# Seven-product gate in two more token groups of a fused attention and SwiGLU kernel, with stores and the q weighting moved to other engines

## The chip, the cores and the metric

The kernel runs on one core of a Trainium2 chip. The metric is the device time of one execution in microseconds (us); the time before is the median of three runs. The profile is of one execution, and its times count from the span's start.

## What is computed

A linear attention (cosformer) over 8 batches, 8 heads, 576 positions and 64 features is followed by a SwiGLU feed-forward block over the resulting 4608 tokens of 512 features. Cut to what matters:

```python
def phi(x, c, s):                      # c, s: cosine and sine of the position, per position
    r = np.maximum(x, 0.0)
    return np.concatenate([r * c, r * s], axis=-1)
q_p, k_p = phi(q, cos_w, sin_w), phi(k, cos_w, sin_w)
kv = np.einsum('bhsf,bhsd->bhfd', k_p, v)
z = np.sum(k_p, axis=2)
num = np.einsum('bhsf,bhfd->bhsd', q_p, kv)
den = np.einsum('bhsf,bhf->bhs', q_p, z)[..., None] + 1e-06
x = (num / den)                        # heads joined: 4608 tokens x 512
g = x @ w_gate                         # 512 x 1536
h = g / (1 + np.exp(-g)) * (x @ w_val) # w_val: 512 x 1536
out = h @ w_out                        # 1536 x 512
```

## The kernel before

The tokens are worked through in nine groups (0 to 8) of 512 tokens. A group has an FFN stage (12 chunks of 128 hidden features: gate and value products, silu, multiplication) and an output stage. Work for later groups is put into slots between the chunks: 12 slots in the FFN stage (0 to 11) and 4 in the output stage (12 to 15). Batch b's q, k and v are prepared so that its key-value products run in slot 5 of group b - 1, and each group's four token tiles (the attention result x and its transposition xT) are made during the group before.

PSUM is eight banks that the program hands out itself with `take` and `give_back`; a helper may take a bank that an earlier user has still to be read from, and then TensorE waits.

A plain group's chunk:

```python
def ffn_mm(...):
    for i in which:                    # gate, then value
        for kc in range(KC):           # 4 matmuls of 512 tokens each
            nc.tensor.matmul(out=..., lhsT=(wg_sb, wv_sb)[i][:, kc, fs], rhs=xT[tg][:, ts, kc], ...)
```

Groups in `GATE` (7 and 8 before) compute the gate by a scheme with seven block products in place of eight (of the Strassen-Winograd kind), in three thirds u of four chunks each. It needs weight sums (made once, `gate_weight_sum`), differences of xT (`x_sum`, in the output stage of the group before) and additions of partial results:

```python
def product(to, u, a, x, first):       # 4 matmuls of 256 tokens
    ...
for u in range(3):
    product(a, u, A11, B11, True)
    b = bank("b", seeded=True)
    nc.scalar.copy(out=b, in_=a)                                        # seeds bank b
    product(e, u, W3, X3, True)
    nc.scalar.copy(out=m7, in_=e)
    V(...); done()                     # V: value product of a chunk; done: a slot
    product(b, u, W2, X2, False)
    nc.vector.tensor_tensor(out=c, in0=m7, in1=b, op=ALU.add)           # L659
    product(a, u, A12, B21, False); silu(u, 1, 0, a)
    mul(...); V(...); done()
    product(b, u, W1, X1, False)
    nc.vector.tensor_tensor(out=m7, in0=m7, in1=b, op=ALU.add)          # L668
    silu(u, 0, 1, m7)
    product(c, u, A22, X4, False); silu(u, 0, 0, c)
    V(...); done()
    # ... mul x2, token sums in the last third
    product(b, u, W4, B22, False); silu(u, 1, 1, b)
    # ... V, mul, done, and the token sum S3 (second third) or S4 (last third)
```

Here `product` is L621, `V` is L633, `silu` is L627 and `mul` is L638. The output stage of groups 2 to 8 (`out_by_quarters`, matmuls L786) is a scheme of the same kind, with seven products of 12 matmuls of 256 columns, in the order a, e, b, slot 12, a, slot 13, b, c, slot 14, b, slot 15. It uses the sums S1 to S4 of the hidden values, made by VectorE (`token_sum`, L760). Its third b product needs S4, and VectorE to have read bank b for the quarter C22 (L827).

The preparation of q on ScalarE and VectorE, and the copies of the key-value result:

```python
def phi_q(b, g):                       # one of 4 head pairs
    relu_op("act", o, o)                                                # ScalarE, L266
    nc.vector.tensor_tensor(out=st[b, "q"][:, g], in0=o..., in1=tab, op=ALU.mult)   # VectorE, L283
def vmul(b, g):                        # v weighted by cosine and sine, VectorE, L287
def qturn_dma(b, e):                   # DMA transpose of st[b, "q"] (tile r_q, one buffer) into phit
    nc.sync.dma_start_transpose(...)
def kv_out2(b):                        # four copies PSUM to SBUF, L356
    for w, eng in enumerate((nc.scalar.copy, nc.vector.tensor_copy)): ...
def store(t, cols=..., queues=None):   # two stores of a tile's rows
    (queues or (nc.sync, nc.sync))[e].dma_start(...)
def load_behind(b):
    nc.gpsimd.tensor_copy(out=hold2, in_=phit[b - 1][0:1, :, 0, 0, 0])  # waits for the turned q of b - 1
    load(b, "q")
    if b > 3:
        load_kv(b)
```

Loads are issued from GpSimd's queue; stores and DMA transposes are issued from SyncE's queue, in program order.

Of the kernel before, what the change touches and what calls it, by code (L numbers as in the profile page):

```python
# [18 lines left out]
def kernel(  # L19
# [29 lines left out]
    HT = T // 2  # L49
    HD = d_model // 2  # L50
    KH = KC // 2
    GATE = (7, 8)

    consts = ctx.enter_context(tc.tile_pool(name="consts", bufs=1))
    raw = ctx.enter_context(tc.tile_pool(name="raw", bufs=2))
# [221 lines left out]
    def phi_q(b, g):  # L277

        if g == 0:
# [3 lines left out]
        nc.vector.tensor_tensor(out=st[b, "q"][:, g], in0=o.unsqueeze(2).to_broadcast([P, NC, 2, D]),  # L283
                                in1=tab, op=ALU.mult)

    def vmul(b, g):
        nc.vector.tensor_tensor(  # L287
            out=v2s[b == 1][:, g, :, :, 0:D],
            in0=(first if b == 0 and g == 0 else {"v": raw_of(b, "v")})["v"][:, g].unsqueeze(2).to_broadcast([P, NC, 2, D]),
            in1=tab, op=ALU.mult,  # L290
        )
# [59 lines left out]
    def kv_out2(b):  # L351

        ps = st[b, "kvps"][:, :, 0:4 * J * D1 // 2].rearrange("p e (j w x) -> p e j w x", j=J, w=2)
        for w, eng in enumerate((nc.scalar.copy, nc.vector.tensor_copy)):
            for i in range(2):
                eng(out=kv2s[b % 2][w * D:(w + 1) * D, :, :, i], in_=ps[i * D:(i + 1) * D, :, :, w])  # L356

# [249 lines left out]
    def ffn_by_quarters(tg, slot_of):  # L607
# [37 lines left out]
        for u in range(3):  # L645
            a = bank("a", fills=True)
            product(a, u, A11, B11, True)
            b = bank("b", seeded=True)
            nc.scalar.copy(out=b, in_=a)
            e = bank("e", fills=True)  # L650
            product(e, u, W3, X3, True)
            m7 = m7p.tile([P, 2, HT], FP32, name="m7")
            nc.scalar.copy(out=m7, in_=e)
            free("e")
            V(*((u - 1, 1, 1) if u else (u, 0, 0)))
            done()
            product(b, u, W2, X2, False)
            c = bank("c", seeded=True)
            nc.vector.tensor_tensor(out=c, in0=m7, in1=b, op=ALU.add)  # L659
            product(a, u, A12, B21, False)  # L660
            silu(u, 1, 0, a)
            free("a")
            if u:
                mul(u - 1, 1, 1)
            V(u, 0, 0) if u else V(u, 1, 0)
            done()
# [3 lines that stand above are left out]
            product(c, u, A22, X4, False)  # L670
            silu(u, 0, 0, c)
            free("c")
            V(u, 1, 0) if u else V(u, 0, 1)
            done()
            if u == 2:
                for n in (1, 2):
                    token_sum(n, 0, 4)
            mul(u, 0, 0)
            mul(u, 1, 0)
            if u == 2:  # L680
                token_sum(3, 4, 6)
            product(b, u, W4, B22, False)
            silu(u, 1, 1, b)
            free("b")
            if u:
                V(u, 0, 1)
            mul(u, 0, 1)
            if u:
                done()
                token_sum(*((3, 0, 4) if u == 1 else (4, 0, 4)))  # L690
        V(2, 1, 1)
        mul(2, 1, 1)
        for n in (1, 2):
# [73 lines left out]
    def out_by_quarters(tg, slot_of):  # L767

        last = tg == NTG - 1
        t0 = tg * OUT  # L770
        for t in (t0, t0 + 2):
            ob_of(t)
# [41 lines left out]
        product(b, S2, T2, False)  # L814
        for p_, o_, x_ in each(b, c[0], C22):
            nc.vector.scalar_tensor_tensor(out=o_, in0=x_, scalar=UP, in1=p_, op0=ALU.mult, op1=ALU.add)
        token_sum(4, 4, 6)
        slot_of(0)
        product(a, aq[:, 1, 0], bq[:, 1, 0], False)
        copied("act", C11, a)  # L820
# [12 lines left out]
        if last:  # L833
            store_two(t0 + 2, slice(0, HD))
        else:
            for t in (t0 + 2, t0 + 3):
                store(t)
        slot_of(2)
        product(b, S4, bq[:, 1, 1], False)
        copied("dve", C12, b)  # L840
        free("b", nb)
        for t in (t0, t0 + 1):
            store(t, *((slice(HD, d_model), (nc.sync, nc.scalar)) if last else ()))
        slot_of(3)

# [149 lines left out]
    def load_behind(b):  # L996

        nc.gpsimd.tensor_copy(out=hold2, in_=phit[b - 1][0:1, :, 0, 0, 0])  # L998
        load(b, "q")
        if b > 3:  # L1000
            load_kv(b)

    def load_kv(b):
        for nm in ("k", "v"):
# [13 lines left out]
    for b in range(2, B):  # L1018
        s0 = SLOTS * (b - 1)
        keng = "dve" if b == 2 else "act"  # L1020
        steps = [lambda b=b, g=g: phi_q(b, g) for g in range(G)]
        steps += [lambda b=b, g=g: (relu_k(b, g, g + 1, keng), vmul(b, g)) for g in range(G)]
        if b == 2:
            fs, tq = [s0 + i for i in (0, 0, 1, 1, 4, 5, 5, 6)], (s0 + 2, s0 + 2)
        else:
            p0 = s0 - SLOTS
            fs, tq = [p0 + 12, p0 + 12] + [p0 + 11 + i for i in range(2, 8)], (p0 + 15, p0 + 16)
            if b == 3:
                fs, tq = [p0 + 12 + i for i in range(4)] + [s0 + 4, s0 + 4, s0 + 5, s0 + 5], (s0 + 2, s0 + 2)
            at(p0 + 3 if b < 5 else p0 + 1, lambda b=b: load_behind(b))  # L1030
        tk = (s0 + 4, s0 + {2: 8, 3: 7}.get(b, 5))
        for s, f in zip(fs, steps):
            at(s, f)
# [4 lines left out]
    for t in range(2 * OUT, NTG * OUT):  # L1038
# [9 lines left out]
        else:  # L1048
            if t in (13, 14, 15):
                s = SLOTS * 2 + t - 4  # L1050
            elif tg - 1 in GATE:
                s = SLOTS * (tg - 1) + ((1, 2, 7, 9) if tg < 6 else (1, 2, 4, 7) if tg < 8 else (1, 2, 5, 6))[i]
            at(s, lambda t=t: a_tile2(t), turn(t))
    for tg in range(1, NTG):
        s0 = SLOTS * tg
# [46 lines left out]
```

## Time and profile before

| what | value |
|---|---|
| time, median of 3 (lowest to highest) | 316.58 us (316.38 to 317.22) |
| profiled span | 314.5 us, mean granted TensorE clock 0.998 |
| plain chunks' matmuls (L564) | 368 + 368, 173.2 us |
| silu of plain groups on ScalarE (L570) | 92, 51.5 us |
| multiplication in plain groups on VectorE (L575) | 92, 57.9 us |
| q weighting on VectorE (L283) | 24, 17.6 us |
| v weighting on VectorE (L287) | 27 + 4, 22.7 us |
| stores from SyncE's queue (L711, L718) | 67 of 128 KB, 2.5 us from issue to landing |
| loads of q, k, v by GpSimd's queue | 6.0, 8.8, 11.4 us from issue to landing |
| DMA engines' share | 0.8 to 1.0 in groups 3 to 5, under 0.4 from group 6's output stage on |

The busy time of an engine in the profile is the time in which it executes; matmuls are pipelined, so the time between two of them, 0.216 us for 512 columns and 0.109 us for 256, is shorter than the duration that a row gives. The chain of waits is followed back from the last instruction, so what it lists are the pieces of work that set the end. A row of the groups gives the line, the engine, the tiles, the shapes, the count, then the busy time and the mean duration, then the idle time before it and what ended it. A row of a timeline gives the start, the duration and in brackets the idle time ahead with its releaser.

### The profile page before, as it was taken

How to read it: one execution, taken by the hardware profiler on the slowest of the kernel's cores; microseconds unless marked ns; L12 is line 12 of the kernel's file. 1: busy time of each engine (PE TensorE's matmuls, PEld its weight loads, DVE VectorE, ACT ScalarE, POOL GpSimd, SP SyncE). 2: the span in 40 equal slices, each digit the busy share in tenths (PEclk: the TensorE clock that was granted, in tenths of full speed). 3: DMA queues.
4: the chain of work that ended last, by engine and by line, in shares of the span. 5: the costliest groups of instructions: out<-in, count | busy, mean ns of one | idle time of the engine just before them, and what ended most of it. 6: DMA issues, size and time to landing. Idle time of an engine off the chain costs nothing.

```text
span 314.5 us, 6775 instructions
## 1 busy us (share of the span) xinstructions
PE 307.5 (98%) x2696; PEld 189.7 (60%) x2696; DVE 228.2 (73%) x458; ACT 143.4 (46%) x264; POOL 36.0 (11%) x62
## 2 busy tenths in 40 slices
PE   8899999999999999999999999999999999999994
PEld 4597455455444585548654764577456866687673
DVE  7873777697678888587748786778779478946772
ACT  7554545763335346334543454335533345324530
POOL 7855102000200200030003000300000000000000
PEclk9999999999999999999999999999999999999999
DMA  7999999996897994989495979598951160014004
GB/s 268 217 198 197 206 205 138 226 133 99 143 208 114 150 145 110 148 119 196 100 153 75 200 144 154 73 192 135 164 86 35 40 145 17 20 38 98 0 2 133
DMA packets 74767, 41.07 MB, mean 131 GB/s; under 512 B 49904, under 2 KB 69872, under 8 KB 74736
## 3 DMA queue, kind: packets, MB, share of 16 engines
q1 hardware_dynamic: 51952, 22.55, 38.0%
q0 software_dynamic: 22192, 17.57, 37.2%
q10 hardware_dynamic: 592, 0.52, 0.5%
q8 instruction: 21, 0.34, 0.4%
q14 instruction: 10, 0.08, 0.1%
HBM read 37.75 MB, written 9.44 MB: 150 GB/s over the span
## 4 chain that ended last, share of the span: by engine, by line
PE 91%; DVE 5%; ACT 2%; issue 1%; ACTq 0%
PE banks L564 46%; PE banks L786 20%; PE banks L729 6%; PE banks L633 5%; PE banks L621 5%; PE banks L333 3%; PE banks L448 3%; DVE ht L638 1%; PE banks L494 1%; PE banks L430 1%; DVE v L287 1%; DVE sums L760 1%; DVE x L471 1%; PE banks L197 1%; PE banks L536 0%
## 5 line engine op out<-in xcount | busy, mean ns | idle before, releaser
L564 PE MATMUL banks<-xT,wg_sb 128*128 128x512 f16 (+2 forms) x368 | 86.6, 360 | 0.0
L564 PE MATMUL banks<-xT,wv_sb 128*128 128x512 f16 (+2 forms) x368 | 86.6, 360 | 0.0
L570 ACT ACTIVATE sg<-banks 128x512 bf16<-128x512 f32 (+2 forms) x92 | 51.5, 560 | 76.0 <-PE banks L564 74.0
L575 DVE TENSOR_TENSOR ht<-sg,banks 128x512 f16<-128x512 bf16 (+2 forms) x92 | 57.9, 637 | 29.7 <-PE banks L564 22.7
L564 PEld LDWEIGHTS <-wv_sb 128*128 128x128 f16 x368 | 35.5, 98 | 37.4
L564 PEld LDWEIGHTS <-wg_sb 128*128 128x128 f16 x368 | 33.9, 98 | 31.5 <-issue 0.2
L786 PEld LDWEIGHTS <-ht 128*128 128x128 f16 x336 | 32.5, 98 | 4.2
L786 PEld LDWEIGHTS <-sums 128*128 128x128 f16 x252 | 24.5, 98 | 4.2 <-issue 0.8
L633 PE MATMUL banks<-xT,wv_sb 128*128 128x512 f16 x96 | 24.3, 379 | 0.0
L283 DVE TENSOR_TENSOR r_q<-raw_q,tab 128x1152 bf16<-128x1152 bf16 x24 | 17.6, 754 | 7.4 <-ACT raw_q L266 7.1
L729 PE MATMUL banks<-wo_sb,ht 128*128 128x512 f16 x96 | 22.7, 379 | 0.0
L471 DVE TENSOR_TENSOR x<-banks,rec 128x512 f16<-128x512 f32 (+1 forms) x32 | 21.6, 674 | 1.3 <-PE banks L430 0.3
L786 PE MATMUL banks<-wo_sb,ht 128*128 128x256 f16 x168 | 20.6, 273 | 0.0
L287 DVE TENSOR_TENSOR v<-raw_v,tab 128x1152 bf16<-128x1152 bf16 x27 | 19.9, 751 | 0.5 <-ACT raw_v L849 0.5
L786 PE MATMUL banks<-wt_sb,sums 128*128 128x256 f16 x168 | 19.8, 273 | 0.1
L786 PE MATMUL banks<-wt_sb,ht 128*128 128x256 f16 x168 | 19.5, 273 | 0.0
L799 ACT ACTIVATE ob<-banks 128x512 f32<-128x512 f32 x14 | 8.4, 597 | 21.9 <-PE banks L786 21.9
L638 DVE TENSOR_TENSOR ht<-sg,banks 128x512 f16<-128x512 bf16 x24 | 15.5, 681 | 2.4 <-ACT sg L627 2.4
L266 ACT ACTIVATE raw_k<-raw_k 128x576 bf16<-128x576 bf16 (+1 forms) x25 | 17.1, 694 | 0.0
L998 POOL COPY hold<-phit 1x2 bf16<-1x2 bf16 x5 | 1.4, 287 | 129.3 <-DMA phit<-r_q 129.3
L760 DVE TENSOR_TENSOR sums<-ht 128x1024 f16<-128x1024 f16 (+1 forms) x28 | 15.5, 553 | 0.4
L266 ACT ACTIVATE raw_q<-raw_q 128x576 bf16<-128x576 bf16 x24 | 15.4, 675 | 0.0
(121 smaller groups left out, 334.6 us busy)
## 6 DMA issues: line engine op xcount, KB each, us to landing
out_dram<-ob SPq DMA_DIRECT2D x67, 128.0 KB, 2.5
raw_k<-in_k_dram POOLq DMA_DIRECT2D x7, 576.0 KB, 8.8
raw_q<-in_q_dram POOLq DMA_DIRECT2D x6, 576.0 KB, 6.0
raw_v<-in_v_dram POOLq DMA_DIRECT2D x6, 576.0 KB, 11.4
wo_sb<-in_moe_w_out_dram POOLq DMA_DIRECT2D x3, 512.0 KB, 12.8
wg_sb<-in_moe_w_gate_dram POOLq DMA_DIRECT2D x5, 256.0 KB, 9.4
wv_sb<-in_moe_w_val_dram POOLq DMA_DIRECT2D x5, 256.0 KB, 9.5
wo_sb<-in_v_dram SPq DMA_DIRECT2D x2, 576.0 KB, 4.0
```

Of the source, the lines that this page charges most:

```text
L266: nc.scalar.activation(out=out, in_=in_, func=AF.Relu)
L283: nc.vector.tensor_tensor(out=st[b, "q"][:, g], in0=o.unsqueeze(2).to_broadcast([P, NC, 2, D]), in1=tab, op=ALU.mult)
L287: nc.vector.tensor_tensor(out=v2s[b == 1][:, g, :, :, 0:D], in0=(first if b == 0 and g == 0 else {"v": raw_of(b, "v")})["v"][:, g].unsquee ...
L471: nc.vector.tensor_tensor(out=st["x", t].rearrange("p (y e d) -> p e y d", e=2, d=D)[:, :, ys], in0=ps[:, :, 0:2 * J * D1].rearrange("p e ...
L564: nc.tensor.matmul(out=st["f", tg, fc, lo][i], lhsT=(wg_sb, wv_sb)[i][:, kc, fs], rhs=xT[tg][:, ts, kc], start=(kc == 0), stop=(kc == KC - 1))
L570: nc.scalar.activation(out=sg[:, 0:n], in_=st["f", tg, fc, lo][0], func=AF.Silu, scale=DOWN)
L575: nc.vector.tensor_tensor(out=ht[:, fc, r:r + n], in0=st.pop(("s", tg, fc, lo))[:, 0:n], in1=ps[1], op=ALU.mult)
L633: nc.tensor.matmul(out=val[u, i, w], lhsT=wv_sb[:, kc, fc * P:(fc + 1) * P], rhs=xT[tg][:, :, kc], start=(kc == 0), stop=(kc == KC - 1))
L638: nc.vector.tensor_tensor(out=ht[:, fc], in0=gates[u, w][:, i], in1=val.pop((u, i, w)), op=ALU.mult)
L729: nc.tensor.matmul(out=o_ps[t], lhsT=ht[:, fc, r:r + P], rhs=wo_sb[:, fc], start=(fc == 0), stop=(fc == FC - 1))
L760: nc.vector.tensor_tensor(out=o[:, lo:hi], in0=x[:, lo:hi], in1=y[:, lo:hi], op=op)
L786: nc.tensor.matmul(out=to[i][:, 0] if len(to) == 2 else to[0][:, i], lhsT=a[:, kc, i * P:(i + 1) * P], rhs=b[:, kc], start=first and kc == ...
```

## The change

Groups 5 and 6 also get the gate by seven products. To make room for its additions on VectorE, the weighting of q for batches 6 and 7 goes to ScalarE as one step (`relu(scale * x)` with the cosine or sine per partition, 18 small activations for a batch, two in each of the slots 4 to 12 of group b - 2). That needs q earlier, so q of batches 6 and 7 is loaded a batch ahead, and the v weighting moves from the start of group b - 1 into the output stage of group b - 2. In gate groups the key-value copies are all ScalarE's. Two thirds of token sum S4 (four of six chunks) move from the gate's last third to the output stage, the token tiles get other slots, and the stores of groups 3 to 7 are issued from GpSimd's queue, so that they don't stand ahead of the transposes in SyncE's.

```diff
-    GATE = (7, 8)
+    PHI_ACT = 6
+    GATE = (5, 6, 7, 8)
 ...
+    def phi_q_part(b, c, w):
+        if (b, "q") not in st:
+            st[b, "q"] = rel.tile([P, G, NC, 2, D], BF16, name="r_q")
+        nc.scalar.activation(out=st[b, "q"][:, :, c, w], in_=raws[b, "q"][:, :, c], func=AF.Relu,
+                             scale=csk[:, c, w:w + 1])
 ...
-        for w, eng in enumerate((nc.scalar.copy, nc.vector.tensor_copy)):
+        for w, eng in enumerate((nc.scalar.copy, nc.scalar.copy if b - 1 in GATE else nc.vector.tensor_copy)):
 ...
             if u:
                 done()
-                token_sum(*((3, 0, 4) if u == 1 else (4, 0, 4)))
+            if u == 1:
+                token_sum(3, 0, 4)
 ...
+        queues = (nc.gpsimd, nc.gpsimd) if tg > 2 else None
 ...
-        token_sum(4, 4, 6)
+        token_sum(4, 0 if tg in GATE else 4, 6)
 ...
-                store(t)
+                store(t, queues=queues)
 ...
-            store(t, *((slice(HD, d_model), (nc.sync, nc.scalar)) if last else ()))
+            store(t, *((slice(HD, d_model), (nc.sync, nc.scalar)) if last else (slice(0, d_model), queues)))
 ...
     def load_behind(b):
         nc.gpsimd.tensor_copy(out=hold2, in_=phit[b - 1][0:1, :, 0, 0, 0])
-        load(b, "q")
+        if b < PHI_ACT:
+            load(b, "q")
         if b > 3:
             load_kv(b)
+        if PHI_ACT <= b + 1 < B:
+            load(b + 1, "q")
 ...                                    # for each batch b: s0 = first slot of group b - 1, p0 = of group b - 2
-        steps = [lambda b=b, g=g: phi_q(b, g) for g in range(G)]
+        steps = [lambda b=b, g=g: phi_q(b, g) for g in range(G)] if b < PHI_ACT else []
 ...
+            if b >= PHI_ACT:
+                for c in range(NC):
+                    at(p0 + 4 + c, lambda b=b, c=c: (phi_q_part(b, c, 0), phi_q_part(b, c, 1)))
+                fs, tq = [p0 + 12, p0 + 12, p0 + 13, p0 + 15], (p0 + 13, p0 + 13)
 ...                                    # slots of the token tiles
-            elif tg - 1 in GATE:
-                s = SLOTS * (tg - 1) + ((1, 2, 7, 9) if tg < 6 else (1, 2, 4, 7) if tg < 8 else (1, 2, 5, 6))[i]
+            elif tg in GATE:
+                s = SLOTS * (tg - 1) + ((1, 3, 7, 9) if tg < 6 else (1, 3, 5, 7))[i]
```

The four weight sums are spread over the groups up to the first gate group: they were made in the last slot of groups 1, 2, 4 and 5, and are now made in the last slot of groups 1, 2, 3 and 4.

## The prediction

> **What bounds the kernel now.** I read the page's first part first, then its chain.
>
> ```profile
> PE 307.5 (98%) x2696; PEld 189.7 (60%) x2696; DVE 228.2 (73%) x458; ACT 143.4 (46%) x264; POOL 36.0 (11%) x62
> ...
> PE 91%; DVE 5%; ACT 2%; issue 1%; ACTq 0%
> ```
>
> TensorE is busy for 98% of the span, and the chain that ended last runs over it for 91%. So two things can shorten the kernel: fewer matmul columns, or fewer waits of TensorE. Whatever only moves work between VectorE, ScalarE, GpSimd and the queues counts by the waits of TensorE that it makes or ends.
>
> Next I cut the span into stages. In the chain in order of time, the piece "PE banks L786" is always an output stage, and what lies between two of them is the feed-forward (FFN) stage of a group. Busy time of each engine in the stages of groups 5, 6, 7, 8 (FFN, then output; columns: stretch, length, then PE, PEld, DVE, ACT, POOL busy with counts, clock, DMA share, GB/s):
>
> ```profile
> 185.32:208.47 23.15, 23.15 (x202) 11.53 (x203) 18.34 (x35) 9.90 (x18) 2.91 (x4) 1.00 0.82 137
> 208.47:217.83 9.36, 9.33 (x85) 8.17 (x84) 6.40 (x13) 4.94 (x9) 0.00 (x0) 1.00 1.00 150
> 217.83:240.98 23.15, 23.15 (x210) 11.36 (x208) 18.45 (x35) 9.90 (x18) 0.00 (x0) 1.00 0.64 113
> 240.98:250.26 9.28, 9.28 (x88) 8.32 (x87) 4.68 (x11) 2.36 (x4) 0.00 (x0) 1.00 0.10 19
> 250.26:271.55 21.29, 20.86 (x166) 13.78 (x164) 17.43 (x35) 9.90 (x18) 0.00 (x0) 1.00 0.34 75
> 271.55:281.13 9.58, 9.50 (x87) 8.29 (x86) 5.52 (x11) 2.36 (x4) 0.00 (x0) 1.00 0.00 1
> 281.13:300.66 19.53, 19.53 (x134) 12.91 (x133) 13.81 (x23) 9.76 (x18) 0.00 (x0) 1.00 0.24 55
> ```
>
> Groups 5 and 6 have the plain gate, and TensorE never pauses in their FFN stages (23.15 of 23.15). Groups 7 and 8 have the gate by seven products already. Group 8's FFN stage is 19.53 and has no pause either. Group 7, which also builds group 8's four token tiles on VectorE, pauses: 20.86 of 21.29, and its output stage is 0.3 longer than group 6's. There VectorE ends the waits; from the timeline of TensorE and of VectorE:
>
> ```profile
> 257.20 0.60 PE L621 MATMUL banks<-kvt,wgs_sb 128*128 128x256 f16 x4 [0.35 <-DVE x L471]
> ...
> 272.58 0.68 DVE L760 TENSOR_TENSOR sums<-ht,sums 128x1024 f16<-128x1024 f16 x1
> ```
>
> The second line is the sum S4 of the token sums, which stands ahead of the last gate-times-value product (L638) and the small sums that the output stage needs. So group 7 shows what a gate group costs when VectorE is full.
>
> **What the Trainium skill says.** "ScalarE: Activation LUTs", section "What ACT_TABLE_LOAD costs": each operand given per partition adds about 93 ns to an activation. The trace agrees. Of these two rows of the groups by shape, the first has such a scale and is 98 ns longer for the same 260 elements:
>
> ```profile
> L504 ACT ACTIVATE tmp<-banks,cs_all 128x260 f32<-128x260 f32 x10 | 4.6, 475 | 4.2 <-PE banks L494 4.2
> ...
> L381 ACT CAST kvt<-banks 128x260 bf16<-128x260 f32 x3 | 1.0, 377 | 2.1 <-PE banks L373 2.1
> ```
>
> "DMA: Bandwidth & Descriptors", section "Issuing engines are not separate DMA queues": transfers of all queues run on the same 16 engines, and another queue saves only issue time. I use this below; this trace alone doesn't show it. "SBUF — State Buffer", section "SBUF: two separate sides", warns that a VectorE instruction in a two-port mode can keep GpSimd from writing descriptors. The trace shows no sign of it: at 170.10 to 172.33, with VectorE busy nearly all the time, GpSimd's three load issues took 0.74, 0.75 and 0.76 us.
>
> **The change part by part.**
>
> *Gate in groups 5 and 6.* A plain group's gate is 48 matmuls of 512 columns; the chain has 48 of them in 10.36 us. Seven products of 12 matmuls of 256 columns are 84; the chain has 8 in 0.87, so 9.14 us. That saves **1.2 us a group**, all of it on the path. Check: a plain FFN stage is 96 x 0.216 = 20.7, group 8's is 19.53. For both groups: **-2.4**. An unpaused FFN stage of group 5 or 6 would then be 19.53 + 1.18 (the key-value products, L333) + about 1.15 (four token tiles) = 21.85.
>
> *What it adds to VectorE in each.* Six additions from PSUM (L659, L668) at about 0.69, and four differences of xT (L605) at about 0.42: 5.8 us. What goes: the weighting of q for batches 6 and 7 (four times 0.754, from the output stages of groups 4 and 5), and the two copies of the key-value result (0.86). The v products (four times 0.75) move from the next FFN stage into the output stage of groups 4 and 5, where the q products stood. So VectorE in the FFN stage of groups 5 and 6 has group 7's work (17.4) less S4 (0.68): 16.7 of 21.9. It fits as a sum, but the order has waits as in group 7. I allow 0.75 a group.
>
> *What it adds to ScalarE.* Per gate group six copies at about 0.58 = 3.5. The q weighting is 18 activations of 256 elements with a scale per partition. From 576 elements in 675 ns and 1152 in 1156, the slope is 0.835 ns an element, so 256 elements need 408, plus 98: about 0.5 us each, some 0.4 when back to back, since activations in a row overlap (two L627 take 1.07 where one takes 0.60). That is 7.2 us for batch 6 in group 4 (plain, ScalarE was 9.9 of 23: room) and for batch 7 **in group 5**, where ScalarE then has 9.9 + 7.2 + 0.75 (two more key-value copies) = 17.9 of about 23. The order of the built program shows where it hurts: in the second third of group 5 ScalarE has, between the end of the key-value products and the copy that seeds the third third's bank b, four key-value copies (1.25 overlapped), three pairs of q (2.4, one ahead of them) and a silu. Followed through by hand with these durations, the copy ends about 0.7 after TensorE wants it.
>
> *Start of group 5.* On VectorE the last weight sum (0.95, L597) now stands between group 4's last eviction and the difference X2. X2 is ready about 0.6 + 0.9 + 0.4 + 0.2 = 2.1 after the stage's end, TensorE wants it at 0.44 + 0.44 + 0.86 = 1.74: a wait of 0.4. Group 5 in all: 21.85 + 0.75 + 0.7 + 0.4 = 23.7, against 23.15: **+0.5**. Group 6: 21.85 + 0.75 = 22.6: **-0.55**.
>
> *Output stage of group 5.* S4 is now made whole there (0.95 instead of 0.42), and three v products (about 2.0) stand ahead of the update of C22, which TensorE's last product waits for. 0.2 + 0.6 + 0.9 + 2.0 + 0.6 = 4.3 after the b product, and TensorE is there after 3 x 1.31 = 3.9: **+0.4**. Group 4's keeps the short S4 and three products in the same place: 0. Group 6's has no v products: 0.
>
> *Groups 7 and 8.* S4 leaves the crowded end of the FFN stage: of group 7's 0.5 to 0.7 of pauses and the 0.3 in its output stage I take back half: **-0.5**. Group 8 has no pause to lose: -0.1.
>
> *Stores on GpSimd's queue, and q a batch ahead.* Nothing on the chain waits for a store or a load of q in groups 3 to 7, so by itself 0. It serves the order of SyncE's queue: batch 5's transposes of q were issued at 157.79, behind eight store issues of 5.82. Now they can go at about 153.3 and land near 164 to 165. That matters, since the first q activation of batch 6, in group 4 at about 162, rewrites the same buffer (one r_q): ScalarE waits some 2 us there. Plain groups have PSUM banks for two or three chunks ahead, so I expect nothing on TensorE.
>
> Sum: +0.5 - 0.55 + 0.4 - 0.5 - 0.1 = -0.25, so 316.3; since some of my pauses may overlap with each other, I put it at **315.9**.
>
> **The rivals.** (1) *The full gain*: ScalarE, VectorE and PSUM have enough slack, as in group 8. -2.4 and -0.8 from groups 7 and 8: 313.4. For it: sums of busy time fit in every stage. Against: group 7 paused with a sum that fitted. (2) *ScalarE becomes the bound in group 5*: q pairs at 0.8 in nearly every slot, with the key-value copies. If every third of the stage slips by a microsecond, group 5 is 3 us longer and the kernel at 318 to 319. (3) *A transfer is late*: the transposes of q or the loads of k and v now stand behind stores and holds on GpSimd's in-order queue ("POOL hold L998" waited 129.3 us in five waits already). k and v of batch 6 should land near 176, v is used near 180, so there are about 4 us of room; a slip beyond would show as TensorE waiting in groups 4 to 6 and cost 1 to 4 us. (4) *Transfers are hidden anyway*: then moving the stores brings nothing by itself, which is what I assume.
>
> **Range and chances.** Between rival 1 (313.4) and rival 2 (318.5) lies the range: **313.8 to 318.2**. 2% is 6.3 us, which is more than twice the whole saving of matmul time, so faster by over 2% has 0.01; slower by as much needs a late transfer in several groups: 0.03; within 2%: 0.96.
>
> **What would show it.** Group 5's FFN stage about 23.7 with TensorE waiting about 2 in it, for ScalarE's seeding copy or VectorE; group 6's about 22.6; group 7's under 21.1 and its output stage under 9.5; group 5's output stage about 9.8, with its last product waiting for VectorE; group 8 and groups 0 to 3 unchanged to 0.2; the q activations at 0.5 each. It is wrong if FFN stages 5 and 6 both come out near 21.9 (pauses oversized), if group 5 is beyond 25 (ScalarE undersized), or if groups 3 and 4 change by over 0.5 (transfers, which I put at nothing).

## The result and the profile after

The changed kernel takes 320.36 us (median of four, 320.22 to 320.79), against 316.53 for the kernel before (median of four, the three of the table above among them): a ratio of 1.0119, interval 1.0101 to 1.0137. It is 3.8 us slower, above the end of the predicted range (318.2).

From the page of the changed kernel, the engines and the chain:

```profile
PE 306.1 (96%) x2768; PEld 196.6 (62%) x2768; DVE 230.8 (72%) x462; ACT 159.5 (50%) x308; POOL 57.3 (18%) x102
...
PE 77%; DVE 10%; DMA 5%; ACT 3%; issue 2%; SPq 1%; DVEq 0%; ACTq 0%
```

TensorE is busy for 1.4 us less than before, since the gate needs fewer matmuls, but the span is 3.9 us longer. Its share of the chain fell from 91% to 77%: VectorE has 10% now, and there is a new entry, DMA, with 5%. So the time went into waits of TensorE, in two kinds. The stages tell where they lie. First groups 3 and 4 of the kernel before, which the prediction doesn't show, FFN and output in turn (columns as in the table of the prediction):

```profile
120.31:143.34 23.03, 23.03 (x202) 11.46 (x201) 18.33 (x35) 9.90 (x18) 2.40 (x4) 1.00 0.89 144
143.34:152.70 9.36, 9.33 (x85) 8.17 (x84) 6.40 (x13) 4.94 (x9) 0.00 (x0) 1.00 0.84 136
152.70:175.96 23.26, 23.26 (x211) 11.43 (x209) 17.81 (x34) 9.90 (x18) 2.40 (x4) 1.00 0.79 133
175.96:185.32 9.36, 9.33 (x85) 8.03 (x84) 6.34 (x13) 4.95 (x9) 0.00 (x0) 1.00 0.93 157
```

Then the changed kernel's, from group 3's FFN stage to group 7's output stage:

```profile
120.61:143.87 23.26, 23.26 (x204) 11.69 (x203) 18.57 (x35) 9.90 (x18) 3.14 (x5) 1.00 0.90 145
143.87:154.55 10.68, 9.10 (x82) 7.75 (x80) 7.71 (x15) 5.22 (x9) 2.13 (x5) 1.00 1.13 183
154.55:178.03 23.48, 23.44 (x210) 11.57 (x211) 16.69 (x33) 14.91 (x32) 4.54 (x8) 1.00 1.06 172
178.03:187.30 9.27, 9.27 (x87) 8.27 (x86) 6.84 (x15) 6.06 (x12) 0.49 (x1) 1.00 0.77 102
187.30:211.30 24.00, 22.89 (x238) 14.87 (x236) 18.99 (x37) 16.29 (x35) 5.44 (x11) 1.00 0.80 142
211.30:221.03 9.73, 9.34 (x87) 8.20 (x85) 7.12 (x13) 6.78 (x14) 0.94 (x2) 1.00 0.44 65
221.03:244.48 23.45, 23.00 (x246) 14.94 (x245) 18.25 (x36) 11.36 (x22) 3.25 (x7) 1.00 0.46 92
244.48:253.65 9.17, 9.17 (x87) 8.22 (x85) 5.21 (x10) 2.36 (x4) 0.38 (x1) 1.00 0.01 2
253.65:276.04 22.39, 21.21 (x167) 13.94 (x165) 17.59 (x35) 9.87 (x18) 3.77 (x8) 1.00 0.29 71
276.04:285.21 9.17, 9.17 (x86) 8.21 (x85) 5.20 (x10) 2.36 (x4) 0.39 (x1) 1.00 0.01 3
```

Against before: group 3's output stage is 1.3 longer (it was 9.36), and its FFN stage and group 4's are 0.2 longer; group 5's FFN stage 0.85 and its output stage 0.37; group 6's FFN stage 0.3 longer instead of 0.55 shorter; and group 7's FFN stage 1.1 longer. The output stage of group 7 is shorter by 0.41, group 8's by 0.14, and those of groups 4 and 6 by 0.1. Groups 0 to 2 take 0.3 longer, which is no effect of the change: in e2 (below), whose program is the same up to there, group 3 starts at 120.31 as in the kernel before.

The edges of these stages are pieces of the chain. With edges at the first matmul of each stage instead, up to 0.25 us moves between neighbours: group 3's output stage is then 1.75 longer and the FFN stages of groups 3 and 4 are as before; group 7's FFN stage is 0.94 longer and its output stage 0.25 shorter.

The wait before group 4 is in the chain, as the piece "DMA xT<-x" (first two lines), and in TensorE's timeline:

```profile
146.21 8.33 DMA xT<-x
154.54 0.05 issue
...
154.59 1.04 PE L571 MATMUL banks<-xT,wg_sb 128*128 128x512 f16 x4 [1.59 <-DMA xT<-x]
```

The transposition of group 4's last token tile was issued at 146.21 and landed 8.33 us later, while the DMA engines' share was over 1; group 4's first matmul waits 1.59 us for it. In the kernel before, the same transposition was issued at 145.92 and landed in 4.7 us. It is the stretch in which batch 6's q is now loaded as well.

Behind it, a second wait is building up, on ScalarE:

```profile
167.02 0.91 ACT L290 ACTIVATE r_q<-raw_q,cs_all 128x256 bf16<-128x256 bf16 x2 [3.29 <-DMA phit<-r_q]
```

ScalarE's first q part for batch 6 writes r_q, which batch 5's transposes are still reading until 167, so ScalarE stands for 3.29 us with group 4's silus behind that part. Here it costs TensorE nothing; the experiments show why.

In the gate groups VectorE sets most of the pauses. The chain through group 6's first two thirds:

```profile
224.50 0.27 PE banks L455 x8
224.79 0.18 DVE den L465
224.99 0.21 DVE rec L474
225.23 0.69 DVE x L478
225.92 0.61 DVE m L675
226.55 1.12 ACT sg L634 x2
227.69 1.88 DVE ht L645 x3
...
230.53 0.70 DVE banks L666
231.27 1.03 PE banks L628 x8
```

It runs from a token tile's matmuls through the tile's three steps on VectorE (den, rec, x), the gate's addition, the silu, the multiplications and the next tile's steps to the next addition, and only then back to TensorE. In the second third of group 7 (VectorE's timeline, then TensorE's):

```profile
269.60 0.68 DVE L768 TENSOR_TENSOR sums<-ht 128x1024 f16<-128x1024 f16 x1
270.20 0.16 DVE L465 TENSOR_SCALAR den<-banks 128x8 f32<-128x8 f32 x1
270.39 0.20 DVE L474 RECIPROCAL rec<-den 128x8 f32<-128x8 f32 x1
270.63 0.69 DVE L478 TENSOR_TENSOR x<-banks,rec 128x512 f16<-128x512 f32 x1
271.24 0.69 DVE L666 TENSOR_TENSOR banks<-m,banks 128x512 f32<-128x512 f32 x1
...
271.98 0.60 PE L628 MATMUL banks<-kvt,wgs_sb 128*128 128x256 f16 x4 [0.22 <-DVE banks L666]
```

A token tile (den, rec, x: 1.04 us from 270.20 to 271.24) stands ahead of the gate's addition L666, and TensorE's b product waits for that addition. (L666 and L675 here are L659 and L668 of the kernel before.)

### The profile page after: what moved, and what is told of

Same layout as the page of the kernel before. It is cut to its first block, busy times and chain, and to the rows that moved or that the text cites. A ratio compares the mean times of both kernels' runs of the same rounds, so it can differ in the third digit from the quotient of the medians. Undisturbed runs are those within 1.5% of the kernel's fastest.

```text
span 318.4 us, 6948 instructions
## 1 busy us (share of the span) xinstructions
PE 306.1 (96%) x2768; PEld 196.6 (62%) x2768; DVE 230.8 (72%) x462; ACT 159.5 (50%) x308; POOL 57.3 (18%) x102
## 4 chain that ended last, share of the span: by engine, by line
PE 77%; DVE 10%; DMA 5%; ACT 3%; issue 2%; SPq 1%; DVEq 0%; ACTq 0%
PE banks L571 32%; PE banks L795 16%; PE banks L640 9%; PE banks L628 7%; PE banks L737 6%; PE banks L340 3%; DMA xT<-x 3%; DMA ht<-in_k_dram 3%; DVE ht L645 2%; PE banks L455 2%; DVE x L478 2%; ACT sg L634 1%; DVE sums L768 1%; DVE banks L666 1%; DVE rec L474 1%
## 5 line engine op out<-in xcount | busy, mean ns | idle before, releaser
L571 PE MATMUL banks<-xT,wg_sb 128*128 128x512 f16 (+2 forms) x272 | 62.1, 354 | 1.6 <-DMA xT<-x 1.6
L571 PE MATMUL banks<-xT,wv_sb 128*128 128x512 f16 (+2 forms) x272 | 62.0, 354 | 0.0
L577 ACT ACTIVATE sg<-banks 128x512 bf16<-128x512 f32 (+2 forms) x68 | 37.1, 546 | 48.5 <-PE banks L571 47.6
L582 DVE TENSOR_TENSOR ht<-sg,banks 128x512 f16<-128x512 bf16 (+2 forms) x68 | 41.5, 620 | 25.7 <-PE banks L571 14.0
L640 PE MATMUL banks<-xT,wv_sb 128*128 128x512 f16 x192 | 48.6, 379 | 0.3 <-DVE ht L645 0.3
L719 POOL DMA_DIRECT2D out_dram<-ob x40 | 20.9, 531 | 109.4 <-ACT ob L808 109.4
L645 DVE TENSOR_TENSOR ht<-sg,banks 128x512 f16<-128x512 bf16 x48 | 30.8, 681 | 6.3 <-ACT sg L634 6.3
L634 ACT ACTIVATE sg<-banks 128x512 bf16<-128x512 f32 x36 | 20.4, 589 | 14.1 <-PE banks L628 14.1
L628 PEld LDWEIGHTS <-wgs_sb 128*128 128x128 f16 x192 | 17.9, 97 | 10.4 <-issue 3.8
L628 PE MATMUL banks<-kvt,wgs_sb 128*128 128x256 f16 x144 | 21.6, 272 | 1.3 <-DVE banks L666 0.7
```

Source lines behind the costliest of these rows:

```text
L571: nc.tensor.matmul(out=st["f", tg, fc, lo][i], lhsT=(wg_sb, wv_sb)[i][:, kc, fs], rhs=xT[tg][:, ts, kc], start=(kc == 0), stop=(kc == KC - 1))
L577: nc.scalar.activation(out=sg[:, 0:n], in_=st["f", tg, fc, lo][0], func=AF.Silu, scale=DOWN)
L582: nc.vector.tensor_tensor(out=ht[:, fc, r:r + n], in0=st.pop(("s", tg, fc, lo))[:, 0:n], in1=ps[1], op=ALU.mult)
L628: nc.tensor.matmul(out=to[:, i], lhsT=a[:, c, 2 * u + i], rhs=x[:, :, c], start=first and i == 0 and c == 0, stop=c == KH - 1, skip_group_ ...
L634: nc.scalar.activation(out=gates[u, w][:, :, j * HT:(j + 1) * HT], in_=src, func=AF.Silu, scale=DOWN)
L640: nc.tensor.matmul(out=val[u, i, w], lhsT=wv_sb[:, kc, fc * P:(fc + 1) * P], rhs=xT[tg][:, :, kc], start=(kc == 0), stop=(kc == KC - 1))
```

## Experiments

Stage sums of the profiled runs, each from the start of one output stage to the start of the next, so that a group's FFN stage stands with the output stage before it. The first column runs from the start of group 3's FFN stage to group 4's output stage. Ratio is to the kernel before. The stages are of the profiled execution, whose own time is over 1 us off the median in two rows: 320.54 in e4, the slowest of its four, and 321.13 in e7, the fastest.

| run | time | ratio (interval) | 3 and 4 | 5 | 6 | 7 |
|---|---|---|---|---|---|---|
| before | 316.5 to 316.8 | 1 | 55.65 | 32.51 | 32.51 | 30.57 |
| changed | 320.36 | 1.0119 (1.0101 to 1.0137) | 57.42 | 33.27 | 33.18 | 31.56 |
| e1_q6_late | 327.27 | 1.0324 (1.0298 to 1.0350) | 64.85 | 33.27 | 33.19 | 31.56 |
| e2_last_tiles | 319.22 | 1.0096 (1.0059 to 1.0133) | 57.43 | 33.28 | 33.18 | 30.62 |
| e3_stores_sync | 324.63 | 1.0255 (1.0236 to 1.0275) | 62.29 | 33.28 | 33.19 | 31.56 |
| e4_plain_5_6 | 318.75 | 1.0076 (1.0047 to 1.0105) | 59.65 | 32.22 | 32.45 | 31.49 |
| e5_tiles_behind | 321.96 | 1.0167 (1.0152 to 1.0182) | 57.54 | 5 to 7: 99.8 | | |
| e6_tiles_early_3 | 323.92 | 1.0212 (1.0176 to 1.0249) | 60.97 | 33.27 | 33.73 | 31.36 |
| e7_no_q6_load | 322.85 | 1.0188 (1.0157 to 1.0219) | 58.45 | 33.28 | 33.18 | 31.56 |
| c1_both_moves | 324.00 | 1.0236 (1.0218 to 1.0255) | 59.22 | 5 to 7: 99.8 | | |
| r1_two_rq | 319.78 | 1.0092 (1.0076 to 1.0109) | 57.46 | 33.28 | 33.19 | 31.56 |
| r2_two_rq_early | 318.30 | 1.0051 (1.0036 to 1.0066) | 55.85 | 33.28 | 33.72 | 30.69 |
| r4_two_rq_plain_5_6 | 316.00 | 0.9977 (0.9962 to 0.9992) | 55.79 | 32.22 | 32.46 | 30.61 |
| s1_no_tiles_6_8 | 311.41 | 0.9828 (0.9812 to 0.9844) | 56.06 | 31.89 | 30.54 | 28.70 |
| s2_no_q_in_5 | 318.79 | 1.0063 (1.0044 to 1.0082) | 55.66 | 33.02 | 33.73 | 30.70 |
| c2_gate6_two_tiles | 316.73 | 1.0002 (0.9989 to 1.0014) | 56.32 | 32.74 | 32.79 | 30.62 |
| c3_gate6_three_tiles | 315.11 | 0.9947 (0.9934 to 0.9961) | 55.98 | 33.15 | 30.87 | 30.62 |

The three groups of the changed kernel, 5 to 7, sum to 98.0. Group 3's FFN stage, 23.03 from first matmul to first matmul before, runs up to 23.7 in the first column (c2, where TensorE waits there for batch 4's transposed q), so a few tenths in that column are not read. Two runs that aren't in the table, r3_only_s4 and s3_gate_alone, are told below.

### The transfers: e1, e3, e6, e7

e1_q6_late loads batch 6's q later:

```diff
-        if PHI_ACT <= b + 1 < B:
+        if PHI_ACT < b + 1 < B:
             load(b + 1, "q")
 ...
+            if b == PHI_ACT:
+                at(p0, lambda b=b: load(b, "q"))
```

> The changed kernel, but batch 6's q is loaded at the start of group 4 (slot 0), not in group 3 behind batch 5's loads. Theory T1 (the extra 576 KB load in group 3 keeps the DMA engines full until 154 and makes group 4's last token transposition land 8.3 us after its issue, for which TensorE waits 1.6 us): that wait goes, group 3's output stage is back from 10.7 to about 9.3, and the kernel is at 318.6 to 319.1. Rival R1 (the stores on GpSimd's queue hold the transposition up): no change, 320.4. Rival R3 (the load is late again and ScalarE's first q activation waits for it in group 4): group 3's stage back, group 4's longer by as much.

It took 327.27. The wait before group 4 went, as T1 has it, but something like R3 came in its place, and far larger. ScalarE's timeline, then TensorE's:

```profile
172.85 0.91 ACT L290 ACTIVATE r_q<-raw_q,cs_all 128x256 bf16<-128x256 bf16 x2 [10.61 <-DMA phit<-r_q]
...
175.01 0.21 PE L455 MATMUL banks<-kv,phit 128*64 128x65 bf16 x1 [6.12 <-DVE ht L582]
```

It isn't the load that comes late for ScalarE but batch 5's transposes: the load of q and the stores run beside them, SyncE's queue spends 16.13 us on the two (10.34 in the changed kernel), and they land at 172.9 instead of 167.0. ScalarE waits 10.61, the silus behind it come late, and TensorE waits for banks that haven't been read.

e3_stores_sync puts the stores back: `queues = None`.

> The changed kernel, but all stores are issued from SyncE's queue as before. T1: group 3's output stage stays near 10.7, since batch 6's q is still loaded in group 3; batch 5's transposes of q come later again (behind eight stores), so ScalarE waits longer in group 4, which may cost TensorE up to 1 us there: 320 to 321.5. R1 (stores on GpSimd's queue cost the time): group 3's output stage back to 9.4 and group 7 to 21.3, the kernel near 317.5.

It took 324.63, more than expected for T1, and R1 falls: the stores on GpSimd's queue don't cost time, they save 4.3 us here, with one r_q. Batch 5's transposes are issued at 158.07 (changed kernel: 154.06), behind eight stores, land at 170.1, ScalarE waits 6.21 and TensorE 2.0 before group 4 and 2.2 in it, after which the granted clock is 0.75 and 0.82 for 8 us.

e6_tiles_early_3 issues group 4's transpositions earlier, and e7_no_q6_load leaves the extra load out:

```diff
-            elif tg in GATE:
+            elif tg >= 4:
                 s = SLOTS * (tg - 1) + ((1, 3, 7, 9) if tg < 6 else (1, 3, 5, 7))[i]
```

```diff
-        if PHI_ACT <= b + 1 < B:
+        if b + 1 == PHI_ACT:
+            raws[b + 1, "q"] = raws[b, "q"]
+        elif PHI_ACT < b + 1 < B:
             load(b + 1, "q")
```

> The changed kernel, with group 4's token tiles made in slots 1, 3, 7, 9 of group 3 (changed kernel: 5, 7, 9, 11), so that their transpositions are issued some 3.5 us earlier; the load of batch 6's q stays where it is. Theory T1 (the transposition is slow because the DMA engines are full, and TensorE waits because it is issued so late): the wait of 1.6 us before group 4 goes, 318.6 to 319.1; unlike the run with the load moved to group 4, nothing else collides. Rival (the transpositions only end when the loads end, at about 154, whenever they were issued): the wait stays, 320.4.

> The changed kernel, but batch 6's q is not loaded: batch 6 uses batch 5's q from the buffer in place (this leaves out one load of 576 KB and so part of the input). T1: without the extra load in group 3 the last transposition lands in about 6 us and the wait before group 4 goes (1.6 us); batch 5's transposes of q are issued about 1 us earlier and land earlier, so ScalarE waits less than its 3.3 us in group 4: 318.4 to 318.9. Rival (the transposition is slow for another reason, such as the order of SyncE's queue): 320.4.

In both the wait before group 4 is gone from the trace, so both the load and the late issue are needed for it, and the rivals named there fall. In e7 the last transposition, issued at 146.12, lands in 4.2 us. Yet both kernels are slower, 323.92 and 322.85. From ScalarE's timeline of the early tiles, then TensorE's of the run without the load:

```profile
168.73 0.91 ACT L290 ACTIVATE r_q<-raw_q,cs_all 128x256 bf16<-128x256 bf16 x2 [7.00 <-DMA phit<-r_q]
```

```profile
170.27 0.19 PE L455 MATMUL banks<-kv,phit 128*64 128x65 bf16 x1 [1.77 <-DVE ht L582]
```

TensorE starts group 4 at 152.6 and 152.7 in these runs (154.6 in the changed kernel), so ScalarE comes to r_q earlier; batch 5's transposes land no earlier, at 168.7 and 168.1 (167.0). ScalarE waits longer, 7.0 and 6.25 us in place of 3.3, which is more than the free PSUM banks bridge. So in the changed kernel the wait before group 4 hid the one behind it. That made theory T3.

### One buffer or two for r_q: r1, r2

```diff
-    rel = ctx.enter_context(tc.tile_pool(name="rel", bufs=1))
+    rel = ctx.enter_context(tc.tile_pool(name="rel", bufs=2))
     # for room: xtp 3 -> 2, m7p 2 -> 1, smp 3 -> 2
```

> The changed kernel with two buffers for the weighted q (r_q), so that ScalarE's first part for batch 6 needn't wait until batch 5's transposes have read the only one; to make room, two xT buffers in place of three, one m7, two of the small tiles. Theory T3 (behind the wait for the last xT before group 4 lies a second one, ScalarE's wait for r_q, and the first hides part of the second): ScalarE's wait of 3.3 us in group 4 goes, but TensorE still waits 1.6 us before group 4, so 319.8 to 320.5. If the kernel falls to 319 or below, r_q alone was the bound there; if it rises, the fewer buffers cost.

319.78, at the lower edge of what T3 says: ScalarE doesn't wait in group 4 any more, and the stages of groups 3 and 4 are the same, 57.46 against 57.42, since the wait for xT of 1.63 us is still there. The fewer buffers cost nothing that the stages show.

r2_two_rq_early adds the early tiles of e6 and the slots of e2 for group 8's tiles.

> Two buffers for r_q as in the run before, group 4's token tiles early in group 3 (slots 1, 3, 7, 9), and group 8's in slots 1, 2, 5, 6. T3: with r_q free, the early tiles no longer bring a longer wait in group 4, as they did alone (323.9); both waits go, 1.6 to 1.8 us, and group 7's 1.1: 317.3 to 318.0. Rival (the early tiles are slow for another reason, such as VectorE's work in group 3): 319 to 322.

318.30, a little over the expected 317.3 to 318.0. Groups 3 and 4 take 55.85, 0.2 more than before the change: with r_q free, the early tiles take the whole loss there away. T3 stands, and with it the first part of the loss is explained: 1.77 us from transfers. The misfit is in group 6, which became 0.5 longer than in the changed kernel; its trace shows a new wait of 0.61 us of a token tile's matmuls for a multiplication (L645):

```profile
228.06 0.29 PE L455 MATMUL banks<-kv,phit 128*128 128x65 bf16 x4 [0.61 <-DVE ht L645]
```

It comes with the early tiles: e6 has them alone and is at 33.73 too, r1 is not. The banks may be handed out in another rotation then; that this is the reason wasn't tried.

### Where the tiles stand: e2, e5, c1

e2_last_tiles moves group 8's tiles, e5_tiles_behind those of groups 7 and 6 too:

```diff
-                s = ... ((1, 3, 7, 9) if tg < 6 else (1, 3, 5, 7))[i]
+                s = ... ((1, 3, 7, 9) if tg < 6 else (1, 3, 5, 7) if tg < 8 else (1, 2, 5, 6))[i]   # e2
+                s = ... ((1, 3, 7, 9) if tg < 6 else (1, 2, 6, 9) if tg < 8 else (1, 2, 5, 6))[i]   # e5
```

> The changed kernel, but the token tiles of group 8 are made in slots 1, 2, 5, 6 of group 7, as before the change, not 1, 3, 5, 7. Theory T2 (in slots 3 and 7 the tile's three VectorE instructions stand ahead of the addition L666 that the next b product waits for; in slots 2 and 6 they stand ahead of nothing urgent): group 7's FFN stage falls from 22.4 to 20.7 to 21.2, the kernel to 319.0 to 319.5. Rival R2 (group 7 is longer because of the stores on GpSimd's queue, or because banks are handed out otherwise since group 5): group 7 stays above 22.

> The changed kernel, with the token tiles made in slots 1, 2, 6, 9 of groups 5 and 6 (changed kernel: 1, 3, 5, 7) and in 1, 2, 5, 6 of group 7. In slots 2, 6 and 9 no addition of the gate stands right behind the tile's VectorE work. Theory T2 (in slots 3 and 7 the tile delays L666, for which TensorE's b product waits): group 7 gains the 1.1 that it gained alone (22.4 to 21.2), groups 5 and 6 gain 0.4 to 0.8 each (24.0 to about 23.4, 23.45 to about 22.8), kernel 317.8 to 318.6. Rival R4 (the pauses in groups 5 and 6 come from the sum of VectorE's work, wherever the tiles stand): groups 5 and 6 stay within 0.2, kernel at 319.2.

> The tiles of groups 6 to 8 in slots that delay no addition and those of group 4 early, together. If the two causes add: the changed kernel's 320.4 less 1.6 less 1.9 to 2.4, so 316.4 to 317.1: about the kernel before the change. If they share a cause: no better than the better of the two.

e2 did what T2 says: group 7 gave back 0.94 and the kernel came to 319.22. So 0.94 of group 7's loss is the new slots, which is all of it with edges at the first matmuls. But e5 gave the reverse in groups 5 and 6: 321.96, with 5 to 7 at 99.8 against 98.0. The waits only went elsewhere, among them into the output stage (TensorE's timeline):

```profile
212.62 0.28 PE L795 MATMUL banks<-wo_sb,ht 128*128 128x256 f16 x1 [0.55 <-DVE ht L645]
213.22 0.94 PE L795 MATMUL banks<-wo_sb,ht 128*128 128x256 f16 x7 [0.31 <-DVE ht L645]
```

The tile in slot 9 pushed the token sums and the last multiplications back, and the output stage waits for those. So T2 in its narrow form, that slots 3 and 7 are the fault, falls for groups 5 and 6. c1_both_moves, e5 with e6's early tiles, was 324.0, no better than either: it has the wait for r_q and the misplaced tiles.

### Is it the gate: e4, r4, s3

e4_plain_5_6 and r4_two_rq_plain_5_6 keep the gate of groups 5 and 6 plain, with all else as changed (e4) and as in r2 (r4):

```diff
-    GATE = (5, 6, 7, 8)
+    GATE = (7, 8)
+    PLACED = (5, 6, 7, 8)      # for the key-value copies and, in e4, the tiles' slots
```

> The changed kernel, but groups 5 and 6 keep the plain gate; loads, stores, q on ScalarE, v products, token tiles and key-value copies stand as changed. If the seven-product gate brings anything in groups 5 and 6, this is slower than the changed kernel; T2 (the pauses in these groups eat it): group 5's FFN stage about 23.2 against 24.0, group 6's 23.2 against 23.45, so about 1 us faster than the changed kernel, 319.0 to 319.6, of which the rest over 316.5 is the load of q (1.3 to 1.6) and group 7 (1.1). If it comes to 316.5 or below, the gate in groups 5 and 6 is the whole loss.

> As the run with two r_q buffers and early tiles, but groups 5 and 6 with the plain gate. The gate in 5 and 6 alone stands between the two: if its pauses eat more than the 2.4 us of matmuls it saves, as 320.4 against 318.75 says, this one is 1 to 2 us faster than its counterpart: 315.6 to 316.6. If it is slower, the earlier comparison was spoiled by the wait for r_q.

e4 took 318.75 and r4 316.00. e4's profiled execution also had the wait for r_q (59.65 in groups 3 and 4), but its other three, 318.44 to 318.76, fit the stages of groups 5 to 7 alone: they are 1.85 shorter than the changed kernel's, which makes 318.5. r4 stands clean against r2: it is 2.3 us faster, and the stages agree (1.06 in column 5 and 1.26 in column 6). So the seven-product gate in groups 5 and 6, which saves 2.4 us of matmuls, costs 2.3 net: about **4.7 us of pauses** in r2, and by e4's 1.85 about 4.2 in the changed kernel, whose group 6 is 0.5 shorter. The two windows of group 6's FFN stage, r2 then r4:

```profile
219.38:243.38 24.00, 23.00 (x247) 14.98 (x245) 18.35 (x36) 11.36 (x22) 3.27 (x7) 1.00 0.48 90
```

```profile
217.94:241.21 23.27, 23.27 (x211) 11.45 (x209) 16.32 (x31) 8.66 (x16) 3.80 (x8) 1.00 0.44 95
```

The plain one has no pause; without its pauses the gate one would take about 21.85, by the prediction's estimate.

s3_gate_alone goes the other way, the kernel before with `GATE = (5, 6, 7, 8)` alone.

> The kernel before with nothing changed but the gate by seven products also in groups 5 and 6: q and v weighting, key-value copies, stores and loads as they were. VectorE then has about 18.4 + 5.8 = 24.2 us in group 5's FFN stage of 21.9 without pauses. If VectorE's sum is the bound: stage 5 and stage 6 (24.2 less the q and v work that group 6 has not) come to 25 to 26 and 23.5 to 24.5, the kernel to 318.5 to 321. If it comes to 316 or below, the moves that should make room were the loss.

321.25, ratio 1.0139 (1.0124 to 1.0155). Columns 5 and 6 are about 35.5 and 34.1, so 4.6 together over before, where r2's are 2.0 over. So the moves that make room on VectorE do their work, some 2.6 us of it, but not enough.

### Which engine: s1, s2

s1_no_tiles_6_8 leaves the token tiles of groups 6 to 8 out, s2_no_q_in_5 the q parts of batch 7; both start from r2.

```diff
+            if tg >= 6:                                                # s1
+                at(s, lambda tg=tg: xT.__setitem__(tg, xT[5]))
+                continue
 ...
-                for c in range(NC):                                    # s2
+                for c in range(NC if b == PHI_ACT else 0):
```

> The run with two r_q buffers and early tiles (318.3), but the token tiles of groups 6, 7 and 8 are left out: these groups use group 5's xT (their attention result isn't computed; the gate, value and output products all stay). If the tiles' VectorE work is what pauses the gate groups, as group 8 (no tiles, no pause) suggests: group 6's FFN stage falls from 24.0 by the tiles' own 1.15 of TensorE and by nearly all of the pauses of 2.1, to 20.7 to 21.1, group 5's from 24.1 to 21.2 to 21.8 (its start and ScalarE remain), group 7's from 21.5 to 19.6. If the pauses come from the key-value copies, ScalarE or the banks: group 6 stays above 22.

> The run with two r_q buffers and early tiles (318.3), but batch 7's 18 q parts on ScalarE in group 5 are left out (its transposes read batch 6's weighted q). If ScalarE bounds group 5: its FFN stage falls from 24.1 to 23.2 or below. If VectorE's order does: 23.8 to 24.1, as group 6, which has no q parts and is 24.0 as well; kernel 318.0 to 318.4.

Without the tiles, group 6's FFN stage (first line) and group 7's (second):

```profile
218.24:239.05 20.81, 20.81 (x206) 13.89 (x205) 14.57 (x24) 11.30 (x22) 3.25 (x7) 1.00 0.36 79
...
248.22:267.75 19.53, 19.53 (x134) 12.91 (x133) 13.81 (x23) 9.76 (x18) 3.76 (x8) 1.00 0.20 55
```

No pause is left in either. Group 6 fell by 3.2, of which 1.15 are the tiles' matmuls: the pauses of 2.0 came with the tiles, that is with some 3.8 us of VectorE's work (18.35 to 14.57) put between additions that TensorE waits for. Key-value copies, ScalarE's load and the banks of the gate are all still there. What s1 doesn't tell apart is VectorE's work and the two PSUM banks that each tile takes: of r2's pauses, 0.61 us is a tile's matmuls waiting for a bank. In group 5 the stage fell to 22.68, less than expected: without the tiles ScalarE is next, with a wait of 1.30 us for the copy that seeds bank b.

s2 confirms the order of the two. Without the q parts ScalarE has 11.35 us of work in group 5's FFN stage in place of 16.30, and the stage is 23.81 in place of 24.07. The kernel's time didn't fall with it: 318.79, over the expected 318.0 to 318.4; the profiled execution has 0.7 us more than r2's behind its last matmul, and why stays open.

### Moving the tiles out, nothing left out: c2, c3

From r4, the gate in group 6 as well, and two or three of group 7's tiles made in group 5, which is plain and has room on VectorE:

```diff
-    GATE = (7, 8)
+    GATE = (6, 7, 8)
 ...
-                ... (1, 3, 5, 7) if tg < 8 ...
+                ... (1, 3, 5, 7) if tg < 7 else (-8, -6, 2, 6) if tg < 8 ...    # c2: slots 8, 10 of group 5
+                ... (1, 3, 5, 7) if tg < 7 else (-8, -6, -5, 6) if tg < 8 ...   # c3: slots 8, 10, 11
     # rawq 3 -> 2, xtp 2 -> 3
```

> From the 316.0 version (two r_q buffers, early tiles, plain gate in 5 and 6): the gate by seven products in group 6 as well, with two of group 7's four token tiles moved out of group 6's FFN stage into the plain group 5 (slots 8 and 10), the others in slots 2 and 6; three xT buffers, two for raw q. If the tiles' VectorE work is what a gate group can't bear, group 6's FFN stage is 21.4 to 22.2 in place of 23.3, group 5's 23.6 in place of 23.0, and the kernel 315.0 to 315.9. If any gate group with key-value copies pauses, group 6 stays at 23 and the kernel is 316.3 or more.

> As the run before, with three of group 7's tiles in group 5 (slots 8, 10, 11) and only one in group 6 (slot 6). Tiles as cause: group 6's FFN stage 21.0 to 21.5, group 5's 23.9 to 24.3 (VectorE 16.2 + 3.2 of it, with the token sums in slots 7 to 11 close by): 314.7 to 315.8. If VectorE then gets late in group 5's output stage instead, the gain is given back there: 316.

c2 is at 316.73, no better than before, and its group 6 is 23.60, with TensorE busy for 22.26; with tiles in slots 2 and 6 it still pauses. c3 is at **315.11**, ratio 0.9947 (0.9934 to 0.9961), faster than the kernel before and the changed one. Its FFN stages of groups 5 and 6:

```profile
186.23:210.19 23.96, 23.96 (x227) 12.34 (x227) 17.11 (x35) 14.52 (x32) 5.53 (x11) 1.00 0.88 162
...
219.38:241.06 21.68, 21.62 (x222) 14.23 (x221) 15.52 (x27) 11.37 (x22) 3.79 (x8) 1.00 0.53 90
```

Group 5 takes the three tiles without a pause, and group 6 has VectorE at 15.5 of 21.7 and waits for some 0.6 us: s1's 20.81 and about 0.29 for the one tile's matmuls would make 21.1. From c2 to c3 only one tile moved, from slot 2 to group 5.

### S4 alone: r3

> The kernel before, with only the token sum S4 of the gate groups 7 and 8 moved to the output stage, as in the change. Group 7's output stage was 0.4 shorter with the change, group 8's 0.14, nothing else is touched: 315.9 to 316.3, same as before or 0.1 to 0.2% faster. If it is slower, S4 then comes late for the third b product.

316.31, ratio 0.9991 (0.9976 to 1.0005): at the upper edge of the expected band, and not to be told from no change. Its trace has a wait of 0.57 us for a transposed tile before group 5, where this run changes nothing, so the kernel before has little room for a late transposition too.

## Why the prediction was wrong, step by step

The prediction's terms sum to -0.25, the stages to +3.94 (added up at the end of this section). The gap of 4.19 is 1.77 from groups 3 and 4 (predicted 0), 1.08 from group 7 (+0.58 for -0.5), 0.82 from group 5's output stage and group 6's FFN stage (+0.67 for -0.15), 0.26 from group 4's output stage and group 5's FFN stage (+0.76 for +0.5) and 0.3 from groups 0 to 2, less 0.04 for group 8.

**Transfers at nothing: this step failed first, and cost most.** The prediction named q's load "by itself 0", put batch 5's transposes at 164 to 165 and expected "nothing on TensorE". The load made a transposition land in 8.33 us, and the transposes landed at 167.0. The term is 1.77 us (57.42 against 55.65; r2 takes it back to 55.85). Its own sign of being wrong here, groups 3 and 4 changing by over 0.5, came true. Rival 3 had the size roughly right, "a transfer is late" at 1 to 4 us, but named the transposes of q and the loads of k and v behind GpSimd's queue; what TensorE waited for was group 4's last xT, issued in slot 11 and without a slot to spare. The 2 us of waiting on ScalarE were 3.3, and the thought that PSUM would bridge the wait held only since TensorE was late itself: 6.25 were too many (e7).

**The pauses of a gate group: the right mechanism, mis-sized.** 0.75 us was allowed, taken from group 7 of the kernel before. Group 6 of the changed kernel has 23.45 - 21.85 = 1.6, and 24.0 - 21.85 = 2.1 in r2. The sum of VectorE's work was too low as well: 16.7 was predicted, 18.25 measured in group 6 and 18.99 in group 5. There was no S4 to take off group 7's 17.4, since it ran at 272.58, behind that stage's end at 271.55; and one v product (0.75) stays in both stages, in group 5 also the weight sum (0.95). Even 18.99 fits into 24.00: "it fits as a sum" was the trap that the text itself had warned of in rival 1. s1 shows that the pauses come with the tiles.

**Group 7 at -0.5: wrong in sign.** The output stage did gain, 0.41 (and group 8's 0.14, predicted 0.1). But the FFN stage lost 1.1, because the change also gave group 8's tiles other slots, 3 and 7 for 2 and 6, and the prediction priced nothing for that. e2 puts 0.94 of it on these slots; the rest is the edge between the two stages.

**Group 5: nearly right.** 23.7 was predicted, 24.00 measured. Inside, the parts differ: the seeding copy cost 0.34, not 0.7, the start of the group 0.25, not 0.4, and VectorE's pauses the rest; ScalarE had 16.29 us of work in the stage, not 17.9. That ScalarE was not the bound while VectorE was (s2) speaks against rival 2, though s1 shows it close behind. The output stage's +0.4 was +0.37, by the wait named:

```profile
219.55 1.47 PE L795 MATMUL banks<-wo_sb,sums 128*128 128x256 f16 x12 [0.39 <-DVE ob L836]
```

**Right as well**: the 1.2 us a group of matmul time (group 8 stays at 19.53 without a pause, s1's group 7 reaches 19.53); the q activation at 0.5 us, with 98 ns for its scale given per partition (about 93 by the Trainium skill's "ScalarE: Activation LUTs", section "What ACT_TABLE_LOAD costs"); 500 ns were measured:

```profile
L290 ACT ACTIVATE r_q<-raw_q,cs_all 128x256 bf16<-128x256 bf16 x36 | 16.1, 500 | 3.3 <-DMA phit<-r_q 3.3
```

and that stores on GpSimd's queue do no harm: their 40 issues took 531 ns each. What they bring was underrated; e3 shows 4.3 us.

By stages: 1.77 (transfers) + 0.76 + 0.67 (columns 5 and 6) + 0.99 - 0.41 (group 7) - 0.14 (group 8) + 0.3 (groups 0 to 2) = 3.94, the 3.9 us between the spans.

## What to carry to other kernels

An engine's busy sum doesn't say that added work is free: where TensorE and another engine hand each other work several times within a few microseconds, as in this gate, work in the second engine's queue can delay the hand-over in one slot as in another (e2 gained 0.94, e5 lost 1.8), so move it into a stage without such hand-overs before adding the cheaper products. When a load is moved into a stretch where the DMA engines are full, look for the transfer that is issued last and needed first, and for buffers that a slow transfer keeps from being rewritten. And a wait that is removed may only uncover the next one: remove both before the first is judged.

## What the runs showed of the hardware

After a long pause of TensorE the granted clock fell. In e1, TensorE was idle for most of 169 to 176, and the clock was 0.70 from 172 to 176 and 0.50 from 176 to 180:

```profile
176.00:180.00 4.00, 4.00 (x22) 1.73 (x23) 2.95 (x6) 3.78 (x9) 0.00 (x0) 0.50 1.21 208
```

Four matmuls of 512 columns took 1.89 us there instead of 1.03. With e6's pauses, most of 168 to 172, the clock was 0.57 from 172 to 176. So a pause can cost a second time, a point that the Trainium skill's "TensorE: Matmul & The Clock Gate", section "HAM oscillation — how this bites in real kernels", makes, with a limit of about 3.4 us for idle gaps. Here less was enough: e3's pauses in group 4, 1.73 us at the longest and 2.2 in all, were followed by 0.75 and 0.82 over 8 us. It isn't certain at that length: pauses of 2.3 us in all in e7's profiled execution weren't followed by a lower clock (1.00 from 172 to 180), nor was the changed kernel's wait of 1.6 us.

A DMA transposition of a token tile of 128x512 landed in 2.5 us at the median (2.4 to 9.3) of the eight issued between 199 and 244 us in the kernel before. The four of group 3, around loads of 1.7 MB, took 3.6 to 9.2 us there, and 4.0 to 9.6 in the changed kernel with loads of 2.3 MB; the last of the four, issued some 8 us after the loads, took 4.7 and 8.3.
